# An attention-and-MLP kernel: k of the last six chunks transposed by DMA, in a new fixed order of the work

## The chip, the cores and the metric

The kernel runs on one core of a Trainium2 chip. The metric is the time of one execution in microseconds (us) on the device; the profile adds a trace of one execution. TensorE (PE) does matrix products and transposes, VectorE (DVE), ScalarE (ACT) and GpSimd (POOL) work on elements, SyncE (SP) issues most DMAs. Each engine takes its own instructions in the order in which the program lists them, and waits on semaphores for the others.

## What is computed

A linear attention with a decaying state, and a channel MLP on what it gives. Inputs are r, k, v of shape (4 batches, 8 heads, 768 tokens, 48) in float32.

```python
state = zeros(B, H, 48, 48)
for t in range(768):
    cur = einsum('bhd,bhe->bhde', u * k[t], v[t])
    y[t] = einsum('bhd,bhde->bhe', r[t], state + cur)
    state = w * state + einsum('bhd,bhe->bhde', k[t], v[t])
x = y, heads side by side: (4, 768, 384)
xn = (x - mean(x)) / sqrt(var(x) + 1e-6) * g_ln
out = x + maximum(xn @ w_ch1, 0) @ w_ch2      # 384 -> 1536 -> 384
```

## The kernel before

**Chunks.** The 768 tokens of a batch are cut into 6 chunks of 128, so there are 24 chunks, numbered 0 to 23; chunk i is part i % 6 of batch i // 6. Within a chunk the recurrence becomes products of matrices, and only a state Z passes from a chunk to the next of its batch.

**The words.** Each piece of work has a name with its chunk's number, which this document calls a word. For chunk i they are, in the order of their dependences (lines in brackets):

- `k`, `v`, and `r` for a pair of chunks: loads, issued by SP [180, 186]. Seven buffers each for k and v.
- `sck`: k scaled by powers of w into one of four bf16 buffers [361]; `scr{e}0`, `scr{e}1`: the same for the pair e of r [364].
- `TK`: four TensorE transposes of 128x128 into the PSUM bank `tr` [379]; `kT`: the copy of that bank to SBUF [383]. `TR` and `rT` are the same for r, a pair at a time, in the same bank [394, 400].
- `q`: r times k, elementwise, both transposed [411]; `cc`: its product with u, on PE [438]; `cp` copies that out [449]; `Vb`: v times cp, on POOL [453].
- `at`: eight score products of kT and rT on PE [418]; `A`: the scores times the mask, from PSUM, on DVE [428].
- `vc`: v cast to bf16 [370]; `kv`: the chunk's state product on PE [469, and 460 where Z is carried in by a product]; `S` and `Z`: the state added and decayed [484, 493, 497].
- `y`: A times v, and rT times Z, on PE [521, 509]; `x`: y plus Vb, with the row sum, on DVE [534].
- `xn`: x centred, on ACT or DVE [552, 548]; `sq`, `rs`: the variance and its root [561, 572, 575].
- `ln`, `lc`: xn transposed into xT. For chunks 0 to 7 on TensorE with a copy [605, 617]; from chunk 8 on `lc` is a DMA transpose issued by SP [613].
- `up{g}_{m}`: the first MLP product of group g, part m [630]; `re{g}_{m}`: its relu, on ACT or DVE [644, 646]. Groups 0 to 5 are single chunks, 6 to 14 pairs.
- `dn{i}{m}`: a third of the second MLP product [657] (`dh` for halves of the last chunk [689]); `ot`: the result, on DVE [667]; `st`: its store, issued by SP or ACT [678].
- `w1l`, `w2l`, `w1s`, `w2s`: the MLP's weights loaded in thirds (768 KB each) and scaled or cast [208, 212, 343, 345, 355]. `turn`, `vec`, `uw`, `wl`, `WLZ`, `gn`: small constants at the start; uw is two products of 48x4 on DVE [325].

**The order.** The string ORDER [23 to 67] lists all words once, in an order found beforehand by annealing. A suffix names the engine where there is a choice: `.V` DVE, `.A` ACT, `.G` POOL, `.S` SP. `*n` stands for n filler products on PE. At run time nothing is chosen: each engine gets its words in the order of the string, and SP too, so a DMA that has to wait holds all DMAs behind it on SP. The dependences are declared by `add` [762 to 865].

**KP and QP.** `KP = 24` [590] is the first chunk whose k is not transposed on TensorE, so before all 24 are. For chunks from `QP = 8` to KP, `qp(i)` [405], q reads the PSUM bank of TK itself; for the others it reads the SBUF copy kT:

```python
kT = tk_t[i][:, :HP, :] if qp(i) else kT_t[i][:]
```

For chunks from KP on, `kT` is this on SP, with no TK and no copy; there are four kT buffers in turn:

```python
nc.sync.dma_start_transpose(out=kT_t[i][:], in_=k_bufs[i % NSC].rearrange("p h d -> p (h d)"))
```

Of the kernel before, what the change touches and what calls it, by code (L numbers as in the profile page):

```python
# [20 lines left out]


ORDER = """
r1 k1 k2 Fr0.V k3 v1 v2 w1l2 Fr1.A Fk.A w1l0 scr00.V scr10.G scr11.G r2 scr01.V *18 TR0 rT0.A sck0.V *1 TK0 kT0.A
*1 turn vec uw.V rT1.A sck1.V vc0.V sck2.G *13 at0 *3 TK1 q0.V wl A0 *6 cc0 *1 kv0 kT1.A q1.G WLZ gn TR1 rT2.A *2
y0 at1 rT3.A vc1.A cp0.V Vb0 Z0 sck3.G v3 A1 w1l1 TK2 kT2.V vc2.A cc1 cp1.A kv1 at2 x0 y1 xn0.A ln0 Vb1 q2.G Z1
w1s22.G A2 w1s01.G x1 k4 TK3 kT3.A xn1.A cc2 kv2 lc0.V k5 w1s00.A cp2.V w1s21.G Vb2 scr20.G w1s02.V Z2 w1s20.V v4
w2l0 y2 ln1 lc1.V up0_0 q3.V at3 re0_0.A x2 xn2.V vc3.A up1_0 re1_0.A cc3 up0_2 ln2 re0_2.A sq0 scr21.G A3
w1s12.G lc2.V up1_2 re1_2.V TR2 w1s11.V rT4.V up2_0 y3 sck4.V cp3.A w1s10.A up0_1 re0_1.V Vb3 x3 sck5.G re2_0.A
up2_2 re2_2.V rT5.A TK4 kT4.A q4.G kv3 Z3 up1_1 re1_1.V at4 A4 vc4.G xn3.A w2l1 ln3 up2_1 lc3.A cc4 cp4.A TK5 sq1  # L30
w2s03.V re2_1.A w2s02.G Vb4 up3_2 kv4 w2s01.V rs0 w2s11.G kT5.A w2s00.A y4 x4 xn4.A w2s13.A w2s10.A w2l2 up3_1
re3_1.A w2s20.G at5 dn00 r3 scr31.G q5.V re3_2.V w2s12.V ln4 lc4.V Z4 up3_0 re3_0.A dn01 cc5 v5 w2s23.A w2s22.A
cp5.A Vb5 A5 up4_2 up4_0 w2s21.V dn02 re4_2.A up4_1 scr30.V TR3 sq4 k6 ot0 sq2 sq3 vc5.V y5 r4 re4_1.V k7 rT7.A
rT6.A dn10 dn11 re4_0.A x5 xn5.V ln5 lc5.V dn12 ot1 sck6.G TK6 scr40.G sck7.V up5_0 up5_1 v6 rs1 kT6.A q6.V TK7
kT7.A scr41.V at6 A6 cc6 cp6.A Vb6 dn20 st0.S TR4 q7.V vc6.A kv6 Z6 re5_1.A k8 rT9.A rT8.A dn21 y6 x6 sck8.G at7
A7 dn22 ot2 xn6.A TK8 cc7 cp7.A v7 up5_2 re5_0.A kT8.A re5_2.A vc7.G kv7 S7 Vb7 k10 k9 sck9.G v8 y7 Z7.G x7 xn7.A
r5 dn30 q8 vc8.A at8 A8 v9 k12 dn31 st1.S r6 scr50.G ln6 lc6.V dn32 ot3 cc8 y8 ln7 sq5 lc7.A kv8 S8 dn40 cp8.A
TK9 kT9.A q9 up6_2 dn41 v10 k11 st2.S v12 v13 sq6 scr51.G up6_1 re6_1.A re6_2.A vc9.V sck10.V cc9 cp9.A TR5 Vb8
x8 dn42 rs2 k13 xn8.V lc8 Z8.G scr61.G ot4 Vb9 scr60.G at9 A9 up6_3 kv9 S9 Z9.G dn50 r7 rT11.A rT10.A TK10 q10
sck11.V re6_3.A kT10.A sq7 dn51 y9 x9 up6_4 re6_4.A sck12.V xn9.A lc9 rs3 vc10.G at10 TK11 cc10 q11 kT11.A cp10.A  # L40
up6_0 re6_0.A dn52 A10 up6_5 re6_5.A TR6 st4.A rT13.A rT12.A vc12.G y10 kv10 Vb10 ot5 dn60 at11 dn61 x10 S10
Z10.G cc11 cp11.A A11 xn10.V sck13.G scr70.G v11 vc11.V k15 TK12 kT12.A st5.A dn62 k14 k18 up7_4 at12 re7_4.A
Vb11 up7_5 q12 ot6 re7_5.A sq8 y11 cc12 cp12.A TK13 scr71.G lc10 r8 sq10 dn70 up7_0 up7_2 A12 kT13.V x11 q13
xn11.A lc11 re7_2.V TR7 y12 rT14.A rT15.A vc13.V at13 kv12 Z12 v14 A13 Vb12 up7_1 re7_1.A re7_0.A sq9 sck14.G
# [12 lines left out]
S19 k22 sck22.V v20 y19 x19 rT22.A dn140 up11_1 sq17 re11_1.A dn141 cc20 st13.A cp20.A TK22 kT22.A dn142 at21
up11_0 up11_4 xn18.A vc22.V sck23.V q22 TK23 ot14 xn19.V lc18 lc19 st14.S A21 Z19.G rs8 vc20.G kv20 Vb20 S20
Z20.G re11_0.A kT23.A y20 up11_5 dn150 re11_4.V at23 x20 xn20.V cc21 q23 A23 cp21.A Vb21 re11_5.A up11_2 kv21
dn151 S21 Z21.V up11_3 re11_3.A re11_2.A y21 dn152 sq19 ot15 st15.S cc22 at22 kv22 S22 Z22.G up12_3 dn160 up12_2  # L60
vc23.G A22 x21 cp22.A re12_3.A cc23 dn161 lc20 y23 xn21.V lc21 cp23.A dn162 up12_4 re12_4.A Vb23 re12_2.V up12_1
re12_1.A Vb22 ot16 dn170 up12_5 x23 y22 xn23.A lc23 x22 re12_5.V xn22.V lc22 rs9 dn171 up12_0 dn172 ot17 sq22
up13_0 st17.S re12_0.A up13_5 re13_5.A st7.A re13_0.V dn180 up13_3 re13_3.V dn181 up14_0 re14_0.A sq20 dn182 ot18
up13_4 re13_4.V up13_2 re13_2.A sq23 dn190 up14_3 dn191 up13_1 st18.A re13_1.V dn192 re14_3.A ot19 st19.A up14_4
re14_4.V up14_5 re14_5.A sq21 rs11 rs10 dn200 up14_1 re14_1.A st16.S dn201 up14_2 re14_2.A dn202 ot20 dn210 dh00
dn220 dh01 dn221 dh02 oh0 dn222 ot22 st20.A dn211 dh10 sh0.A st22.A dn212 ot21 st21.S dh11 dh12 oh1 sh1.S
"""


class Planner:  # L70
# [12 lines left out]
    def add(self, name, eng, cost, fn, needs=(), takes=(), gives=(), pri=0, load=0.0, kind=None,  # L83
            alt=None, lands=1.9, after=0.0):

        t = dict(name=name, eng=eng, cost=cost, fn=fn, needs=list(needs), takes=list(takes),
                 gives=list(gives), pri=pri, load=load, kind=kind, alt=alt, lands=lands, end=None,
                 first=(eng, cost), after=after)  # L90
        self.tasks.append(t)
        assert name not in self.by_name, name
        self.by_name[name] = t
# [24 lines left out]
def kernel(  # L118
# [17 lines left out]
    NCH = S // L  # L136
# [106 lines left out]
    NSC, NSR = 4, 2  # L243
# [5 lines left out]
    WLZ = const.tile([P, HP, E2], FP32, name="WLZ")  # L249
# [43 lines left out]
    Fk = const.tile([P, H, D], FP32, name="Fk")  # L293
# [12 lines left out]
    vec = const.tile([P, NR], FP32, name="vec")  # L306
# [3 lines left out]
    wl = const.tile([P, HP], FP32, name="wl")  # L310
# [49 lines left out]
    def scale_k(i, eng):  # L360
        eng.tensor_tensor(out=k_bufs[i % NSC][:, :, :D], in0=k_t[i][:], in1=Fk[:], op=ALU.mult)  # L361
# [10 lines left out]
    def k_bank(i):  # L372
        return "y" if i < 1 else "tr"
# [31 lines left out]
    def qp(i):  # L405
        return QP <= i < KP

# [179 lines left out]
    LNP = 8  # L587
    LNO = 4
    ln_done = []
    KP = 24  # L590
    SZ, QP = 6, 8
    ot_t = {}

# [124 lines left out]
    add = plan.add  # L718
# [22 lines left out]
    for rank, (a, i) in enumerate(seq):  # L741
        pri = 50 - 0.1 * rank
# [19 lines left out]
    for i in range(NT):  # L762
        c = i % NCH
        g, j = tile_group[i]
        last = c == NCH - 1
        p0 = 60 - 2 * i
        e, half = divmod(i, 2)
        add(f"sckb{i}", "", 0.0, None, ([f"TK{i - NSC}"] + ([f"kv{i - NSC}"] if (i - NSC) % NCH < NCH - 1 else [])) if i >= NSC else [], [("sck", i, 1 if last else 2)], pri=p0)
        add(f"sck{i}", "DVE", 0.7, lambda e, i=i: scale_k(i, e), [f"k{i}", "Fk", f"sckb{i}"], [], [("k", i)], pri=p0, after=35 + (i - 6) * PACE if i > 6 else 0.0,
            alt=[("POOL", 1.0)])  # L770
        if not half:
            add(f"scrb{e}", "", 0.0, None, [f"TR{e - NSR}"] if e >= NSR else [], [("scr", e, 1)], pri=p0)
            for t in range(2):
                add(f"scr{e}{t}", "POOL", 1.1, lambda g, e=e, t=t: scale_r(e, t, g), [f"r{e}", f"Fr{t}", f"scrb{e}"], [],
                    [("r", e)], pri=p0, alt=[("DVE", 0.7)])
            add(f"TR{e}", "PE", 0.46, lambda e=e: transposes_r(e), [f"scr{e}0", f"scr{e}1"] + ([f"TK{i - 1}"] if QP < i < KP else []), [("tr", ("r", e), 2)],
                [("scr", e)], pri=p0)
        add(f"rT{i}", "ACT", 0.74, lambda g, i=i: evacuate_r(i, g), [f"TR{e}"] + (["kT0"] if i == 1 else []), [("rT", i, 1)], [("tr", ("r", e))], pri=p0,
            alt=[("DVE", 0.74)])
        if i < KP:  # L780
            add(f"TK{i}", "PE", 0.24, lambda i=i: transposes_k(i), [f"sck{i}"] + ([f"TR{e}"] if qp(i) and i else []), [(k_bank(i), ("k", i), 2 if qp(i) else 1)], [("sck", i)], pri=p0)
# [20 lines left out]
        if not last:  # L802
# [19 lines left out]
            pri=p0 + 2, alt=[("DVE", 0.35)])  # L822
# [78 lines left out]
```

## Time and profile before

| what | value |
|---|---|
| median of 11 runs | 153.42 us (152.78 to 154.24) |
| the profiled execution's own time | 153.73 us |
| its span, first to last instruction | 151.8 us |
| mean granted TensorE clock | 0.989 |
| chain that ended last, by engine | PE 77%, DVE 17%, nothing visible 2%, ACT 1% |
| k transposes on PE (L379) | 96 matmuls, 24 chunks |
| DMA transposes on SP (L613) | 16 |

Busy time counts an engine's instructions; a matmul's end is modelled, so the shares of PE are upper bounds. "Releaser" is what ended an engine's idle time. PEld is the weight load that runs ahead of each matmul. Rows of the timeline give start, duration, engine, source line, operation, output and inputs; the bracket at the end is the idle time before it and what ended that.

### The profile page before, as it was taken

The page shows a single profiled execution, that of the slowest core. Times are in us where ns is not written, and L with a number is a line of the kernel's source. Part 1 is how long each engine was busy: PE and PEld are TensorE (multiplying, and loading weights), DVE is VectorE, ACT ScalarE, POOL GpSimd, SP SyncE. Part 2 cuts the span into 40 slices and gives each one's busy share as a digit, 9 for nine tenths or more (in the row PEclk, how much of TensorE's full clock was granted, in tenths as well). Part 3 has the DMA queues.
Part 4 walks back from the last instruction along what each step waited for, and adds up shares of the span by engine and source line. Part 5 has one row for each costly group of instructions (what it writes and reads, how often), then busy time and mean ns, then how long its engine had stood idle before and what let it go on. Part 6 is the DMA issues. An engine that isn't in the chain of part 4 may idle for free.

```text
span 151.8 us, 4482 instructions
## 1 busy us (share of the span) xinstructions
PE 143.1 (94%) x1778; PEld 112.5 (74%) x1778; DVE 120.8 (80%) x246; ACT 89.0 (59%) x198; POOL 90.1 (59%) x122
## 2 busy tenths in 40 slices
PE   5967899999999999999999999999999999999991
PEld 5856689888677777777778777776867787777770
DVE  5979999998789699899997998679899884535132
ACT  3447567599677676766768554645873526172300
POOL 8087998566687898599817847598384180011200
PEclk9999779999999999999999999999999999999999
DMA  4999998997899994496786898991523121511032
GB/s 97 258 209 324 248 273 160 390 320 166 182 216 238 245 239 122 123 237 126 148 224 150 166 232 166 205 264 58 111 75 101 36 72 30 181 52 52 0 106 107
DMA packets 75563, 25.47 MB, mean 168 GB/s; under 512 B 69648, under 2 KB 74390, under 8 KB 75542
## 3 DMA queue, kind: packets, MB, share of 16 engines
q1 hardware_dynamic: 72966, 23.11, 64.1%
q10 hardware_dynamic: 2480, 2.07, 4.0%
q8 instruction: 14, 0.23, 0.7%
q14 instruction: 7, 0.06, 0.2%
q0 software_dynamic: 96, 0.01, 0.1%
HBM read 18.88 MB, written 4.72 MB: 155 GB/s over the span
## 4 chain that ended last, share of the span: by engine, by line
PE 77%; DVE 17%; issue 2%; ACT 1%; POOL 0%; ACTq 0%; POOLq 0%; DVEq 0%
PE o L657 27%; PE hp L630 26%; PE at L418 4%; DVE A L428 4%; PE tr L379 3%; PE o L259 3%; PE tr L394 3%; PE y L521 2%; PE s L469 2%; PE y L509 2%; DVE vv L370 1%; PE hp L689 1%; DVE x L534 1%; PE hp L657 1%; DVE uwI L325 1%
## 5 line engine op out<-in xcount | busy, mean ns | idle before, releaser
L630 PE MATMUL hp<-xT,w_sb 128*128 128x256 bf16 (+1 forms) x540 | 57.8, 252 | 0.2
L657 PE MATMUL o<-w_sb,hT 128*128 128x384 bf16 x264 | 53.5, 326 | 0.0
L630 PEld LDWEIGHTS <-w_sb 128*128 128x128 bf16 x540 | 43.2, 98 | 7.3 <-ACT w_sb L343 0.4
L644 ACT ACTIVATE hT<-hp 128x512 bf16<-128x512 f32 x54 | 31.9, 598 | 22.1 <-PE hp L630 21.4
L657 PEld LDWEIGHTS <-hT 128*128 128x128 bf16 x276 | 24.5, 97 | 10.5
L428 DVE TENSOR_TENSOR A<-at,mask 128x1024 bf16<-128x1024 f32 x24 | 29.2, 1215 | 1.8 <-PE at L418 1.7
L364 POOL TENSOR_TENSOR sc<-r,Fr 128x384 bf16<-128x384 f32 x19 | 19.7, 1048 | 9.1 <-DMA r<-in_r_dram 9.1
L453 POOL TENSOR_TENSOR Vb<-v,cc 128x384 f32<-128x384 f32 x24 | 20.3, 848 | 7.9 <-ACT cc L449 6.8
L667 DVE SCALAR_TENSOR_TENSOR ot<-o,rs,x 128x384 f32<-128x384 f32 x22 | 13.5, 614 | 8.0 <-PE o L657 7.2
L383 ACT COPY kT<-tr 128x512 bf16<-128x512 bf16 x19 | 11.1, 587 | 12.9 <-PE tr L379 9.9
L400 ACT COPY rT<-tr 128x512 bf16<-128x512 bf16 x20 | 13.9, 744 | 3.8 <-DVE rT L400 1.8
L534 DVE SCALAR_TENSOR_TENSOR x<-y,Vb 128x384 f32<-128x384 f32 x24 | 13.2, 549 | 3.4 <-PE y L521 3.3
L646 DVE TENSOR_SCALAR hT<-hp 128x512 bf16<-128x512 f32 x18 | 12.3, 684 | 4.0 <-PE hp L630 3.8
L561 ACT ACTIVATE sq<-x,sum 128x384 bf16<-128x384 f32 x24 | 14.6, 610 | 1.3 <-DVE x L534 1.3
L361 POOL TENSOR_TENSOR sc<-k,Fk 128x384 bf16<-128x384 f32 x13 | 13.6, 1045 | 0.5 <-DMA k<-in_k_dram 0.5
L572 POOL TENSOR_SCALAR rs<-sqs 128x2 f32<-128x2 f32 x12 | 2.9, 241 | 18.4 <-ACT sq L561 17.8
L493 POOL TENSOR_TENSOR Z<-S,WLZ 128x384 bf16<-128x384 f32 x9 | 9.0, 999 | 7.8 <-DVE S L484 7.8
L379 PE MATMUL tr<-ident,sc 128*128 128x128 bf16 x92 | 9.2, 224 | 2.5 <-DVE sc L361 1.6
L379 PEld LDWEIGHTS <-sc 128*128 128x128 bf16 x96 | 6.6, 100 | 4.2 <-DVE sc L361 2.3
L418 PE MATMUL at<-rT,kT 48*128 48x128 bf16 x192 | 9.5, 219 | 0.0
L575 POOL TENSOR_TENSOR rs<-rs,expo 128x2 f32<-128x2 f32 x12 | 8.5, 710 | 1.0
L521 PE MATMUL y<-vv,A 128*128 128x48 bf16 x192 | 8.8, 185 | 0.2 <-DVE vv L370 0.2
(96 smaller groups left out, 204.7 us busy)
## 6 DMA issues: line engine op xcount, KB each, us to landing
r<-in_r_dram SPq DMA_DIRECT2D x12, 384.0 KB, 4.4
k<-in_k_dram SPq DMA_DIRECT2D x24, 192.0 KB, 4.6
wst<-in_moe_w_ch_dram SPq DMA_DIRECT2D x6, 768.0 KB, 7.5
v<-in_v_dram SPq DMA_DIRECT2D x23, 192.0 KB, 4.3
out_dram<-ot SPq DMA_DIRECT2D x14, 192.0 KB, 2.6
out_dram<-ot ACTq DMA_DIRECT2D x9, 192.0 KB, 2.2
xT<-xn SPq DMA_TRANSPOSE x16, 2.6
v<-in_v_dram ACTq DMA_DIRECT2D x1, 192.0 KB, 3.6
```

Of the source, the lines that this page charges most:

```text
L361: eng.tensor_tensor(out=k_bufs[i % NSC][:, :, :D], in0=k_t[i][:], in1=Fk[:], op=ALU.mult)
L364: eng.tensor_tensor(out=r_bufs[e % NSR][:, j, :, :D], in0=r_t[e][:, :, j * D : (j + 1) * D], in1=Fr[:, j], op=ALU.mult)
L379: nc.tensor.transpose(out=tk_t[i][:, q, :], in_=sc[:, q, :], identity=ident[:])
L400: (eng.copy if eng is nc.scalar else eng.tensor_copy)(out=rT_t[i][:].rearrange("p q (t j) -> p q j t", j=2), in_=tp_t[e][:, :, c * LH : (c ...
L418: nc.tensor.matmul(out=at_t[i][:, par, p, :], lhsT=kT_t[i][p0 : p0 + D, p, :], rhs=rT_t[i][p0 : p0 + D, p, :], start=True, stop=True,)
L428: nc.vector.tensor_tensor(out=A_t[i][:].rearrange("p e q t -> p (e q) t"), in0=at_t[i][:].rearrange("p e q t -> p (e q) t"), in1=mask[:].u ...
L453: nc.gpsimd.tensor_tensor(out=Vb_t[i][:], in0=vf_t[i][:], in1=cc_t[i][:].unsqueeze(2).to_broadcast([P, H, D]), op=ALU.mult)
L534: nc.vector.scalar_tensor_tensor(out=x_t[i][:], in0=y_t[i][:, :C], scalar=1.0, in1=Vb_t[i][:].rearrange("p h d -> p (h d)"), op0=ALU.mult, ...
L561: nc.scalar.activation(out=sq[:], in_=x_t[i][:], func=ACT.Square, bias=sum_t[i][:], scale=-float(C), accum_out=sq_t[e][:, c : c + 1],)
L630: nc.tensor.matmul(out=hp[:, f * gw : (f + 1) * gw], lhsT=w1_sb[:, n, kc, fb * P : (fb + 1) * P], rhs=xT_t[g][:, kc, :gw], start=(kc == 0) ...
L644: nc.scalar.activation(out=out, in_=src, func=ACT.Relu)
L657: nc.tensor.matmul(out=o_t[i][:, :C], lhsT=hT_t[g][:, fk, j * P : (j + 1) * P], rhs=w2_sb[:, fk, :], start=(fk == 0), stop=(fk == FK - 1),)
```

## The change

KP goes from 24 to 18: for chunks 18 to 23 there is no TK, kT is a DMA transpose issued by SP straight from the scaled k, and q reads kT in SBUF. A scaled-k buffer is then free for reuse when that DMA has read it (and kv has). With it the whole string ORDER is replaced by another one: words move and some change engine. Counted over the string, before and after: PE has 24 and 18 TK; fillers 45 and 46; ACT 20 and 14 copies kT, 54 and 51 re, 12 and 15 xn; DVE 18 and 21 re, 11 and 5 sck, 21 and 18 q, 5 and 7 scr; POOL 13 and 19 sck, 3 and 6 q; SP 0 and 6 kT, 14 and 10 st.

The diff, cut; of ORDER the start and the stretch with the six DMA transposes are shown.

```diff
 ORDER = """
-r1 k1 k2 Fr0.V k3 v1 v2 w1l2 Fr1.A Fk.A w1l0 scr00.V scr10.G scr11.G r2 scr01.V *18 TR0 rT0.A sck0.V *1 TK0 kT0.A
-*1 turn vec uw.V rT1.A sck1.V vc0.V sck2.G *13 at0 *3 TK1 q0.V wl A0 *6 cc0 *1 kv0 kT1.A q1.G WLZ gn TR1 rT2.A *2
-y0 at1 rT3.A vc1.A cp0.V Vb0 Z0 sck3.G v3 A1 w1l1 TK2 kT2.V vc2.A cc1 cp1.A kv1 at2 x0 y1 xn0.A ln0 Vb1 q2.G Z1
...
+k1 r1 k2 k3 Fr1.A Fr0.V scr00.V scr01.V w1l2 v1 v2 w1l0 *18 TR0 rT0.V Fk.A sck0.G TK0 sck1.G kT0.A rT1.A vc0.A *1
+turn r2 vec uw.V wl *9 at0 q0.V *5 cc0 A0 scr11.V sck3.V TK1 sck2.G kv0 *10 y0 kT1.A *3 TK2 WLZ at1 A1 kT2.A
+cp0.A scr10.G w1l1 Z0 q1.G TR1 rT2.A at2 rT3.A vc1.A q2.V gn v3 TK3 kT3.A Vb0 x0 A2 vc2.V y1 cc1 cp1.A Vb1 kv1 Z1
+w1s22.A q3.G cc2 xn0.A ln0 at3 w1s01.A cp2.A Vb2 x1 y2 kv2 w1s02.V lc0.V xn1.A ln1 scr20.G w1s00.V w1s21.A
+w1s20.V lc1.V k4 Z2 x2 sq0 scr21.G up0_0 up1_2 A3 w1s11.G re0_0.A xn2.A re1_2.A k5 up1_0 cc3 cp3.V re1_0.A
...
+up8_5 dn91 y14 dn92 cc15 cp15.A Vb15 x14 re8_5.A scr90.G xn14.A q16 rs5 r10 up8_4 re8_4.V lc14 k21 kT18 at16
+up9_5 re9_5.A A16 ot9 y15 up9_2 up9_4 TK17 dn100 x15 sq14 kT17.A kv15 re9_2.V S15 Z15.G dn101 sck19.G at17 dn102
+cc16 vc16.A xn15.A lc15 q17 TR9 st9.A cp16.A scr100.G scr101.G up9_1 ot10 dn110 rT19.V v21 y16 re9_1.V kv16 dn111
+up9_3 kT19 A17 S16 Vb16 sck21.G rT18.A re9_4.A re9_3.V q18.V v18 st10.A up9_0 r11 x16 vc19.V sq12 TR10 cc17
+re9_0.V dn112 ot11 rT20.A cp17.V Z16.V sck20.G kT20 up10_0 at18 A18 q19.V Vb17 sq15 sq13 re10_0.A up10_1 st11.A
+vc18.G dn120 cc18 k23 kT21 v22 y17 dn121 kv18 cp18.A re10_1.A dn122 up10_4 re10_4.A x17 Z18 xn17.A rs6 lc17 ot12
+scr110.V rT21.A st12.A xn16.A lc16 cc19 at19 A19 kv19 S19 y18 up10_2 dn130 scr111.V vc20.V up10_3 Vb18 rs7 x18
+dn131 at20 q20.G A20 sck23.G Z19.G dn132 y19 ot13 k22 sq16 cp19.A Vb19 x19 re10_3.A re10_2.A q21.G up10_5 kT23
+cc20 TR11 at21 vc21.G sq17 re10_5.A cp20.V rT22.V xn18.V A21 dn140 Vb20 y20 sck22.G kT22 q22.G rs8 kv20 dn141 S20
...
-    KP = 24
+    KP = 18
...
-        add(f"sckb{i}", "", 0.0, None, ([f"TK{i - NSC}"] + ([f"kv{i - NSC}"] if (i - NSC) % NCH < NCH - 1 else [])) if i >= NSC else [], [("sck", i, 1 if last else 2)], pri=p0)
+        add(f"sckb{i}", "", 0.0, None, ([f"TK{i - NSC}" if i - NSC < KP else f"kT{i - NSC}"] + ([f"kv{i - NSC}"] if (i - NSC) % NCH < NCH - 1 else [])) if i >= NSC else [], [("sck", i, 1 if last else 2)], pri=p0)
```

## The prediction, made before the changed kernel was run

> **What bounds the kernel now.** I read the page's engine shares first (span 151.8 us), then busy time by stage, then single stretches of the timeline.
>
> ```profile
> PE 143.1 (94%) x1778; PEld 112.5 (74%) x1778; DVE 120.8 (80%) x246; ACT 89.0 (59%) x198; POOL 90.1 (59%) x122
> ```
>
> TensorE (PE) is nearly always busy, but the second engine, VectorE (DVE), has 80% too. So I cut the span into stages; the columns are the stage, its length, and each engine's busy time.
>
> ```profile
> core 0: us, PE busy (x) PEld busy (x) DVE busy (x) ACT busy (x) POOL busy (x), PEclk, DMA share, GB/s
> 7.70:33.10 25.40, 22.30 (x375) 19.10 (x373) 24.19 (x49) 17.07 (x36) 21.24 (x25) 0.93 1.03 276
> 33.10:40.20 7.10, 6.93 (x97) 5.56 (x95) 5.88 (x13) 6.68 (x17) 3.75 (x4) 1.00 0.88 184
> 40.20:105.60 65.40, 65.13 (x841) 49.92 (x839) 57.72 (x111) 42.87 (x94) 49.63 (x63) 1.00 0.82 187
> 105.60:122.10 16.50, 16.25 (x200) 12.50 (x198) 15.36 (x28) 10.05 (x25) 7.74 (x12) 1.00 0.32 82
> 122.10:148.60 26.50, 26.43 (x230) 19.94 (x227) 11.52 (x24) 9.03 (x20) 4.72 (x9) 1.00 0.22 71
> ```
>
> After 33 us PE is full in every stage. Before that DVE is the busiest (24.19 of 25.40). Between 40 and 106 us DVE has only 7.7 us to spare in 65.4.
>
> A busy PE is not a PE at its peak, so I also counted PE's work by the steps from one group's start to the next where nothing waits:
>
> ```profile
> 102.82 0.40 PE L418 MATMUL at<-rT,kT 48*128 48x128 bf16 x8
> 103.15 0.40 PE L379 MATMUL tr<-ident,sc 128*128 128x128 bf16 x4
> 103.38 0.24 PE L438 MATMUL s<-uwI,q 128*128 128x2 bf16 x4
> 103.48 0.36 PE L521 MATMUL y<-vv,A 128*128 128x48 bf16 x8
> ```
>
> The four transposes of one k chunk (L379) take 103.38 - 103.15 = **0.23 us** of PE; the 0.40 shown contains the pipeline's tail, which the next group overlaps. In the same way: at 0.35, cc 0.10, TR 0.45, up and dn 0.66 each, y 0.20 (0.37 with state), kv 0.17 (0.33 with a carried Z), ln 0.17, dh 0.33. Summed over the order's words this is 130.5 us of work. TR0 starts at 7.7 and the last matmul begins at about 148.6, that is 140.9 us, so about 10.4 us are lost. By 33.1 us 17.3 us of work are done in 25.4: **8.1 us are lost there, and only about 2.2 in the 115 us behind it.** From 33 us on a PE microsecond saved is a microsecond of span, as long as DVE keeps up. Below, "mark" means the PE work that stands ahead of a word in the order.
>
> **1. PE work removed.** TK18 to TK23 go: 6 x 0.23 = **-1.38 us**, all of it at marks 75 to 96, in the full stages. Six evacuations kT go too:
>
> ```profile
> L383 ACT COPY kT<-tr 128x512 bf16<-128x512 bf16 x19 | 11.1, 587 | 12.9 <-PE tr L379 9.9
> ...
> xT<-xn SPq DMA_TRANSPOSE x16, 2.6
> ```
>
> Six of these copies are 3.5 us of ScalarE (ACT), which is off the path (59% busy): nothing. The products q18 to q23 read kT in SBUF now, not the PSUM bank tr; the instructions of that line (count, then shortest, median and longest ns) show both forms:
>
> ```profile
> L411 DVE TENSOR_TENSOR q<-rT,tr x16: 406/410/422, 48.6 to 116.6; 128x512 bf16<-128x512 bf16 x16
> ...
> L411 DVE TENSOR_TENSOR q<-rT,kT x5: 418/422/779, 11.8 to 44.2; 128x512 bf16<-128x512 bf16 x5
> ```
>
> 422 against 410 ns on DVE is nothing; q20, q21 and q22 move to GpSimd (POOL).
>
> **2. One stall goes.** TK22 waited in the old order:
>
> ```profile
> 110.01 0.97 DVE L361 TENSOR_TENSOR sc<-k,Fk 128x384 bf16<-128x384 f32 x1 [0.52 <-DMA k<-in_k_dram]
> ...
> 111.04 0.23 PEld L379 LDWEIGHTS <-sc 128*128 128x128 bf16 x4 [0.34 <-DVE sc L361]
> ```
>
> k22 landed late, sck22 followed, and PE stood for about 0.4 us. PE no longer reads sck22 early. Next late is kT22 for at22; see 3. **-0.4 us.**
>
> **3. Six DMA transposes on SP's queue.** The trace has none of this shape. The nearest row is the x transpose of 128x384 shown above: its issue holds SP 1.18 to 2.23 us, median 1.19, and it lands 2.3 to 3.9 us after, median 2.6. For 128x512 the bounds are 0.4 (the shortest plain issue on SP) and 2.23 for the issue, 2.3 and 3.9 x 4/3 = 5.2 for the landing; I take the median row x 4/3, 1.6 and 3.5. From the word kT to its at there are 11.7, 6.9, 8.4, 8.6, 8.6 and 5.4 us of PE work for chunks 18 to 23: each covers 5.2, the last barely. The tile written is that of four kTs before, long read. So no direct wait of PE.
>
> But SP is in order, and a kT waits there for its sck. Behind kT18 stand lc15 and v21, behind kT19 v18 and r11, behind kT20 k23, behind kT21 v22, lc17, lc16 and k22, behind kT23 kT22, then the last lc. v18 is the tight one: already before, the cast of v18 waited for its load,
>
> ```profile
> 98.58 0.50 POOL L370 CAST vv<-v 128x384 bf16<-128x384 f32 x1 [1.65 <-DMA v<-in_v_dram]
> ```
>
> issued at 94.33 (mark 76.9). Now xn15 has mark 73.7 (71.2 before), and lc15, v21 and kT19 (1.2 + 0.6 + 1.6) are ahead of v18, so it issues near mark 78, lands 4.3 later, and with a cast of 0.54 kv18 at 82.6 is late by 0 to 0.6. I take **+0.3**. At chunk 22 POOL runs sck22 and then q22, which waits for kT22's landing; behind q22 stand rs8, vc22, Vb21 and Z21. k22 stands behind lc17 and lc16, whose xn are placed at 84; issued near 88 it lands near 92.6, and this gives q22 done near 98.4 and vc22 near 100, just when kv22 (100.4) wants it: nothing, but 1 to 1.7 us if the landing is at its upper bound.
>
> The Trainium skill, "VectorE: DVE Perf Modes", "The three transpose paths" and "Rules for kernel authors", speaks against the change: a 128x128 bf16 transpose costs 390 ns on TensorE and 1309 ns by DMA, and TensorE is to be used if PSUM will do. By its figures 24 blocks would free 9.4 us of PE and take 31 us of DMA, an estimate; the 0.23 us for four blocks here is far below the first.
>
> **4. The start, reordered.** uw (two tiny products) sits on DVE's path:
>
> ```profile
> 8.07 1.96 POOL L364 TENSOR_TENSOR sc<-r,Fr 128x384 bf16<-128x384 f32 x2 [4.33 <-DMA r<-in_r_dram]
> ...
> 9.03 1.98 DVE L325 TENSOR_TENSOR uwI<-vec 48x4 bf16<-48x4 f32 x2
> ...
> 10.00 0.98 POOL L361 TENSOR_TENSOR sc<-k,Fk 128x384 bf16<-128x384 f32 x1
> ```
>
> Each of the two ends with a POOL instruction (10.0, 11.0), so DVE is held by POOL. The skill's "SBUF — State Buffer", "SBUF: two separate sides", says the two share a port pair that is locked for a whole instruction; the row agrees.
>
> In the new order DVE does scr00, scr01, rT0 (to about 9.1) and uw, while POOL does sck0 (7.3 to 8.35), sck1 (to 9.4), and then wl, which needs uw. So half of uw is free of POOL and it ends near 9.7, not 11.0; then q0 to 10.2, A0 to 11.4, y0 near 11.5 instead of 13.4. It is given back: scr11, two w1s and vc2 now lie on DVE in front of lc1, and w1l2 (768 KB) is loaded ahead of v1 and v2. Going on with row durations I get lc1 done near 21.05 (20.78 before), with up0_0 and at3 behind PE in both orders, and the set up to at4 done near 29.4 against 29.7. **-0.2**, between -1.3 and +1.0, since some 20 handoffs of 0.1 to 0.2 are assumed.
>
> **5. DVE fuller in the middle.** Between marks 24 and 88 (40.2 to 105.6 us before) the new order has on DVE: six more re (683 ns), two vc (797), one each of A (1217), S (552), Z (600), x (630), rT (728), scr (664), two cp (150); fewer: three xn (663), two sck (694), one q (413). That is 10.4 - 3.8 = +6.6 us of durations, about 6.2 after the 6% by which neighbours overlap (61.4 summed, 57.7 busy). So 63.9 us of DVE for about 64.5 of PE. In 70 to 80 us DVE had 9.76 of 10 and PE lost 0.24. At that rate 64 us would cost 1.5; I take **+0.6**, since DVE at 9.34 (60 to 70 us) cost PE nothing. What moves here leaves marks 88 to 104, where DVE gets about 7 us lighter. Bounds: 0 and the +3.3 of rival B.
>
> The tail from dn202 on is the same chain; sq23 and rs11 stand late in the new order, but ACT reaches sq23 some 4 us before oh0 needs it. Nothing.
>
> **Sum:** -1.38 - 0.4 + 0.3 - 0.2 + 0.6 = **-1.1 us**. The profiled execution took 153.73 (span 151.8 and 1.9 around it), 0.3 over the median of the runs, 153.42. From the median: **152.3 us**. Faster and slower count from 0.3% (0.46 us), about what a measurement of this kernel can tell from no change.
>
> **Rivals.**
> A, the forecast: PE stays the bound, 152.3. For it: 2.2 us lost in 115.
> B, **DVE becomes the bound** at marks 24 to 88. Of its 7.7 us of idle time only 0.6 may remain. DVE takes its work in order and so waits for PE now and then; if half the idle time stays (3.9), the stage needs 63.9 + 3.9 = 67.8, 2.4 over 65.4. With the rest of the sum (-0.5 for the TKs beyond, -0.4) it gives 154.9. It makes the kernel slower from 2.4 us of idle on. Against it: DVE that is late finds its inputs ready and idles less.
> C, **the transposes' queue eats the gain**: v18 late by 0.6, the chain k22, sck22, kT22, q22, Vb21 by 0.8, DVE 0.6: about 0 in all, 153.4.
> D, the earlier y0 is kept in good part (1.3 of 1.9): 151.0.
>
> **How the numbers follow.** A 0.46 (0.41 of it faster, 0.05 within), B 0.22, C 0.17 (0.14 within, 0.03 slower), D 0.15. So faster 0.56, same 0.19, slower 0.25. The range takes in most of D and B: 150.7 to 154.9.
>
> **What would show it.** Right: 72 matmuls at L379; the last PE stage as long as before; PE work from 33 us on shorter by 1.4. Wrong: PE idle before y, kv or dn released by DVE between 40 and 106 us (B); POOL idle on DMA for v18 or kT22, or PE at L418 waiting for a transpose (C); PE's first up groups a microsecond earlier or later than 19.8 (D, or the walk in 4).

## The result, and the profile after

| | before | changed |
|---|---|---|
| median | 153.43 us (50 runs) | **155.06 us** (154.24 to 157.06, 13 runs) |
| ratio to before, 95% interval | | 1.0105 [1.0085, 1.0126] |
| the profiled execution's own time | 153.73 us | 154.67 us |
| its span | 151.8 us | 152.6 us |
| mean granted TensorE clock | 0.989 | 0.978 |

The forecast was 152.3, in a range of 150.7 to 154.9. The changed kernel is 1.6 us slower, not 1.1 faster. Executions more than 1.5% above the fastest of their kernel count in the medians of this document and not in its ratios.

The transposes did leave TensorE: L379 has 72 matmuls in place of 96. The page's first line of the changed kernel:

```profile
PE 142.4 (93%) x1755; PEld 112.4 (74%) x1755; DVE 123.7 (81%) x247; ACT 85.5 (56%) x190; POOL 94.9 (62%) x123
```

PE is busy 0.7 us less and the span is 0.8 longer. Busy time by stage, over the stretches that the prediction showed (length, then each engine's busy time, then the granted clock):

```profile
7.70:33.10 25.40, 22.23 (x362) 19.49 (x359) 22.65 (x44) 19.02 (x41) 19.54 (x24) 0.87 1.06 289
33.10:40.20 7.10, 6.24 (x96) 5.13 (x95) 6.40 (x10) 4.80 (x14) 4.88 (x6) 1.00 0.93 200
40.20:105.60 65.40, 64.23 (x821) 49.39 (x819) 60.50 (x116) 39.80 (x91) 49.25 (x62) 1.00 0.91 185
122.10:148.60 26.50, 26.50 (x233) 20.36 (x232) 13.28 (x27) 9.62 (x21) 5.26 (x9) 1.00 0.20 64
```

Three things differ. The clock of the first stage is 0.87 (0.93 before). PE has 0.86 us to spare between 33 and 40 us, where it had 0.17. In the long stage DVE is busy 60.50 us. That row is the same stretch of time and not of work: between the marks of the forecast's stage, 24 and 88, which are 42.1 and 108.1 us here, DVE is busy 61.57 of 66.00, 3.9 more than before and 2.3 less than forecast. The last stage is full in both.

Shares by stage do not say how much each stage lost, since work moved between them. So I made a ledger with the prediction's own steps: the start of a word, less the start of TR0, less the PE work ahead of it (its mark), is the time that PE has lost by then.

| mark | lost before, us | lost after, us | more by |
|---|---|---|---|
| 12.1 | 7.90 | 8.76 | 0.86 |
| 24.5 | 8.56 | 10.58 | 2.02 |
| 49.5 | 9.02 | 11.52 | 2.50 |
| 62 | 9.78 | 12.20 | 2.42 |
| 86 | 9.88 | 12.53 | 2.65 |
| 124 | 10.24 | 12.57 | 2.33 |

2.33 lost less 1.38 of work removed is +0.95 from TR0 on. TR0 itself starts 0.33 us earlier in the changed kernel (7.35 for 7.68), and the two spans differ by 0.8, the two executions by 0.94. **Nearly all of it is lost by mark 24, in the first 42 us; the six DMA transposes come at 92 us and later.** Behind mark 86 the new order loses 0.04 where the old one lost 0.36.

The six transposes themselves, by tile kT in the changed kernel: count and shortest, median, longest issue in ns; who waited; time to landing.

```profile
L387 SPq DMA_TRANSPOSE kT<-sc x6: 1190/1228/1816, 92.1 to 113.2; - x6
...
  POOL q L411: 2.6, 1
...
DMA to landing us min/median/max: 2.4/3.7/5.0
```

PE is not in the list: no score product waited for a transpose in this execution. q22 waited 2.6 us on POOL, and PE was not held by that.

**The start.** uw was freed of POOL, both halves of it where the forecast had one. DVE's timeline of the changed kernel (start, duration, engine, line):

```profile
9.02 0.33 DVE L325 TENSOR_TENSOR uwI<-vec 48x4 bf16<-48x4 f32 x2
...
11.43 1.35 DVE L361 TENSOR_TENSOR sc<-k,Fk 128x384 bf16<-128x384 f32 x1
```

0.33 us in place of 1.98, and y0 began at 11.11 in place of 13.39. But then sck3 took 1.35 us where an undisturbed one takes 0.56, with scr10 on POOL until 12.37 and q1 right behind it. PE stood, between 12.5 and 17.9 us, 0.99 ahead of at2, 0.66 ahead of y1, 0.38 ahead of kv1 and 1.26 ahead of cc2, which wanted Z1, on DVE behind the cast vc2 (0.93). Then the granted clock fell. PE in windows of 2 us, before:

```profile
17.00:19.00 2.00, 1.96 (x25) 0.53 0.75 157
19.00:21.00 2.00, 1.89 (x29) 0.62 0.92 225
21.00:23.00 2.00, 2.00 (x42) 1.00 1.17 328
```

and in the changed kernel (busy, number of matmuls, granted clock):

```profile
17.00:19.00 2.00, 1.15 (x17) 0.50 1.08 359
19.00:21.00 2.00, 2.00 (x27) 0.50 1.15 247
21.00:23.00 2.00, 2.00 (x21) 0.50 0.71 127
```

Half clock lasts from 17.10 to 20.52 before (3.42 us) and from 16.42 to 23.25 after (6.83 us, twice that). Two groups of up in it, up0_0 and up1_2, took 1.28 us each in place of 0.66. A mean clock of 0.978 over the span is two such stretches, 0.989 one. All runs of the changed kernel show 0.973 to 0.978, while runs of the kernel before show from none to two. The Trainium skill, "TensorE: Matmul & The Clock Gate", "What's actually happening", gives a free-running window of 3413 ns after whose idleness PE runs at half rate; both lengths here are multiples of it. But PE was not idle in the 3.41 us ahead of the fall, it was busy 1.63 of them in the changed kernel (below) and 2.16 in the kernel before. In the 3.41 us ahead of those, from 10.28 to 13.69, the kernel before had been busy only 2.04, and its clock stayed up. So the runs bear out the length and not the condition.

```profile
13.01:16.42 3.41, 1.63 (x32) 1.00 1.05 311
```

**Marks 12 to 24.** PE waited 0.78 us ahead of ln4 and 0.53 ahead of ln5. The first of them in the timeline of the changed kernel:

```profile
32.94 1.15 POOL L411 TENSOR_TENSOR q<-rT,kT 128x512 bf16<-128x512 bf16 x1
...
33.12 1.18 DVE L548 TENSOR_SCALAR xn<-x,sum 128x384 bf16<-128x384 f32 x1
...
34.36 0.34 PE L605 MATMUL tr<-ident,xn 128*128 128x128 bf16 x3 [0.73 <-DVE xn L548]
```

xn4 begins on DVE just after q5 has begun on POOL, and ends only after it. By itself it takes 0.5 us (0.52 in a run below). DVE waited for POOL inside the instruction. xn5 takes 0.92 us in the same way, beside scr40.

### The profile page after: what moved, and what is told of

It is laid out like the page before. It is cut to its first block, busy times and chain, and to the rows that moved or that the text cites. A ratio compares the mean times of both kernels' runs of the same rounds, so it can differ in the third digit from the quotient of the medians.

```text
span 152.6 us, 4438 instructions
## 1 busy us (share of the span) xinstructions
PE 142.4 (93%) x1755; PEld 112.4 (74%) x1755; DVE 123.7 (81%) x247; ACT 85.5 (56%) x190; POOL 94.9 (62%) x123
## 4 chain that ended last, share of the span: by engine, by line
PE 76%; DVE 17%; issue 3%; ACT 1%; POOL 1%; POOLq 0%; DVEq 0%; ACTq 0%
PE hp L630 28%; PE o L657 24%; DVE A L428 4%; PE at L418 4%; PE y L521 3%; PE tr L394 2%; DVE xn L548 2%; PE s L469 2%; DVE vv L370 2%; PE y L509 2%; DVE x L534 2%; PE o L259 2%; PE tr L379 2%; DVE sc L361 1%; PE hp L689 1%
## 5 line engine op out<-in xcount | busy, mean ns | idle before, releaser
L630 PEld LDWEIGHTS <-w_sb 128*128 128x128 bf16 x540 | 44.3, 100 | 7.1
L644 ACT ACTIVATE hT<-hp 128x512 bf16<-128x512 f32 x51 | 30.1, 597 | 24.2 <-PE hp L630 24.0
L657 PEld LDWEIGHTS <-hT 128*128 128x128 bf16 x276 | 24.5, 97 | 10.8 <-issue 0.2
L361 POOL TENSOR_TENSOR sc<-k,Fk 128x384 bf16<-128x384 f32 x19 | 19.8, 1046 | 3.9 <-ACT Fk L304 3.4
L646 DVE TENSOR_SCALAR hT<-hp 128x512 bf16<-128x512 f32 x21 | 14.4, 688 | 6.3 <-PE hp L630 6.3
L364 POOL TENSOR_TENSOR sc<-r,Fr 128x384 bf16<-128x384 f32 x17 | 18.4, 1095 | 0.7 <-DMA r<-in_r_dram 0.7
L552 ACT ACTIVATE xn<-x,sum 128x384 bf16<-128x384 f32 x15 | 9.2, 612 | 4.9 <-DVE x L534 3.4
L383 ACT COPY kT<-tr 128x512 bf16<-128x512 bf16 x13 | 7.6, 585 | 5.9 <-PE tr L379 3.6
L493 POOL TENSOR_TENSOR Z<-S,WLZ 128x384 bf16<-128x384 f32 x7 | 7.4, 1061 | 3.1 <-DVE S L484 3.1
L418 PEld LDWEIGHTS <-kT 48*128 48x128 bf16 x192 | 5.5, 95 | 5.1 <-issue 2.0
L411 POOL TENSOR_TENSOR q<-rT,kT 128x512 bf16<-128x512 bf16 x6 | 7.4, 1225 | 2.6 <-DMA kT<-sc 2.6
```

Of the source, the lines that this page charges most:

```text
L364: eng.tensor_tensor(out=r_bufs[e % NSR][:, j, :, :D], in0=r_t[e][:, :, j * D : (j + 1) * D], in1=Fr[:, j], op=ALU.mult)
L418: nc.tensor.matmul(out=at_t[i][:, par, p, :], lhsT=kT_t[i][p0 : p0 + D, p, :], rhs=rT_t[i][p0 : p0 + D, p, :], start=True, stop=True,)
L630: nc.tensor.matmul(out=hp[:, f * gw : (f + 1) * gw], lhsT=w1_sb[:, n, kc, fb * P : (fb + 1) * P], rhs=xT_t[g][:, kc, :gw], start=(kc == 0) ...
L644: nc.scalar.activation(out=out, in_=src, func=ACT.Relu)
L646: nc.vector.tensor_scalar(out=out, in0=src, scalar1=0.0, scalar2=None, op0=ALU.max)
L657: nc.tensor.matmul(out=o_t[i][:, :C], lhsT=hT_t[g][:, fk, j * P : (j + 1) * P], rhs=w2_sb[:, fk, :], start=(fk == 0), stop=(fk == FK - 1),)
```

## The experiments

Times are medians, ratios are to the kernel before on the same chip with the 95% interval. "Lost" is the ledger's figure.

### The DMA transposes in the old order

The first theory was that the transposes are worth their 1.4 us and the new start loses it (T1); the rival, that SP's queue takes the gain (T2). **e1_old_order_dma**: KP = 18 in the old order, each kT right behind its sck.

```diff
-sck18.G ... TK18 kT18.A
+sck18.G kT18
```

So for all six, with v20 and sck23 ahead of sck22.

> The old order with the DMA transposes put into it by hand: KP = 18, no TK18 to TK23, each kT right behind its sck (sck23 moved ahead of sck22 so that kT23 has time). Theory 1 (the transposes do what was reckoned, the loss is in how the new order runs its first 70 us): PE loses 1.38 us of work and the 0.4 us stall at TK22, so 151.3 to 152.2 us, and L379 shows 72 matmuls. Theory 2 (DMA transposes cost more than they save: SP's queue, DMA traffic, late kT): no gain, 153.4 us or more, with PE or POOL idle on kT.

**e2_before_plus_dma**: the kernel before, with the six transposes added behind the same sck into a tile that nobody reads; all 24 TK stay.

```diff
+nc.sync.dma_start_transpose(out=t_[:], in_=k_bufs[i % NSC].rearrange("p h d -> p (h d)"))
```

> The kernel before, all 24 TK kept, and for chunks 18 to 23 one more DMA transpose of the scaled k behind each sck, into a tile that nothing reads. This adds the transposes' cost alone. Theory 1: 153.2 to 153.9 us, as before. Theory 2: the transposes must cost about the 1.6 us that the change lost and the 1.4 us that it saved on PE, so about 156 us, and at least 154.5.

Measured: e1 166.38 us, 1.0783 [1.0725, 1.084]; e2 164.25, 1.0676 [1.0623, 1.073]. By the ratios T1 as it stood missed by 13 us: placed there, the transposes cost 10 us even when nobody reads them and no PE work is saved (e2), and the kernel is 12 us slower with the saving (e1). SP's timeline in e1:

```profile
82.00 0.53 SPq L677 DMA_DIRECT2D out_dram<-ot  x1
85.81 1.88 SPq L386 DMA_TRANSPOSE kT<-sc  x1
87.77 1.21 SPq L612 DMA_TRANSPOSE xT<-xn  x1
```

and PE's:

```profile
90.20 1.16 PE L629 MATMUL hp<-xT,w_sb 128*128 128x256 bf16 x6 [3.51 <-DMA xT<-xn]
```

From 82.5 to 85.8 SP stands before kT18, whose sck18 is only made by then. Behind it is the x transpose of chunk 13, which went out at 82.08 in the kernel before and at 87.77 here, and PE waits 3.51 us for it. What is late here is no k transpose, it is what stands behind one on SP. SP stands before kT20 in the same way, until 110.06, and PE loses 3.1 us more at 116 to 119, where the chain of what it waits for leads back over the landings of two k transposes.

**e5_old_order_dma_timed** and **e8_before_plus_dma_timed** are e1 and e2 with the six at places where the trace of before has the scaled k ready: behind k19, v22, k23, st12 and, two of them, v20, with a few words moved for them (sck20 and sck23; in e5 also q19, q21, q22). In e8 the six are the unread ones.

```diff
-k19 ... v22 ... k23 ... st12 ... sck22 v20 ... sck23
+k19 kT18 ... v22 kT19 ... k23 kT20 ... st12 kT21 ... sck23 sck22 v20 kT23 kT22
```

> KP = 18 in the old order again, but each kT stands on SP's queue at a place where, by the trace of before, its sck has ended (behind k19, v22, k23, st12 and v20), sck20 and sck23 are earlier on their engines, and q19, q21, q22 later on VectorE. Theory 1: what cost 11 us in the first two experiments was SP held by a kT that waited for its sck, with the x transposes and loads behind it; without that the six chunks save 1.4 to 1.8 us: 151.3 to 152.3 us. Theory 2 (the transposes themselves are too slow or disturb other DMAs): 153.4 us or more.

> The kernel before with the six unread DMA transposes of the second experiment, at the places on SP's queue that the run beside this one uses for kT (and sck20, sck23 and v20 moved likewise); all 24 TK stay on PE. Theory 1: the 11 us of the second experiment were the waits on SP's queue, so 153.2 to 154.0 us now. Theory 2: still 155 us or more, as six transposes more are issued in either.

Measured: e5 155.14, 1.0075 [1.0044, 1.0107]; e8 155.47, 1.0132 [1.0091, 1.0173]. Most of the loss has gone, but not all: by the ratios 1.2 us is left in e5 and 2.0 in e8. SP in the kernel before, then in e8:

```profile
91.78 1.21 SPq L613 DMA_TRANSPOSE xT<-xn  x1
...
95.54 1.95 SPq L180 DMA_DIRECT2D r<-in_r_dram  x1
```

```profile
93.53 1.21 SPq L616 DMA_TRANSPOSE xT<-xn  x1
...
99.74 0.58 SPq L179 DMA_DIRECT2D r<-in_r_dram  x1
```

The x transpose of chunk 15 is 1.8 us late and the load of r11 4.2, after two transposes of k. PE loses 3.8 us between 91 and 115 us in the profiled execution of e8 (157.00 us, above its median), where the kernel before loses 0.5. Half of it lies ahead of dn130, which waits for an ot on DVE; and that ot waits for an earlier store, which stands behind r11 on SP, goes out 2.8 us later than before (100.36 for 97.58) and lands 5.29 us after:

```profile
100.36 5.29 DMA out_dram<-ot
...
105.76 0.62 DVE L670 SCALAR_TENSOR_TENSOR ot<-o,rs,x 128x384 f32<-128x384 f32 x1 [2.05 <-DMA out_dram<-ot]
```

**e4_old_then_new**: the order of e1 up to dn70 (mark 52), which holds none of the six, and behind it all other words in the new order.

> KP = 18; the order of the first experiment up to about 52 us of PE work (dn70), and behind it the words that are left in the changed kernel's order. Theory 1: the new order loses PE time only ahead of this point, so 151.3 to 152.4 us, about as the first experiment. Rival (the later stretch with the DMA transposes and the fuller VectorE loses): 154 us or more.

Measured: 155.63, 1.0141 [1.0106, 1.0176]. The seam alone costs about 5 us between marks 53 and 58, so the total tells nothing of the two halves. But from mark 60 on, where the six transposes lie, only 0.4 to 0.6 us is lost. This and the ledger answer T2 for these two executions: at the new order's places the queue costs PE nothing to speak of, and at the old order's it costs 2 to 10 us (e8, e2). That it is not free at the new places either, once PE comes earlier or SP later, e11, e14 and e16 show.

### The clock

**e3_new_order_warm**: the changed kernel with 53 filler products on PE, so that it does not idle at the start.

```diff
-... WLZ at1 A1 ... TR1 rT2.A ... TK3 kT3.A ... cc1 cp1.A ... kv1 Z1
+... WLZ at1 *5 A1 ... TR1 *14 rT2.A ... TK3 *9 kT3.A ... cc1 *5 cp1.A ... kv1 *20 Z1
```

> The changed kernel with 53 filler products on PE, in five places between 11.8 and 18 us where PE stood idle (behind at1, TR1, TK3, cc1 and kv1). Theory 1, in its part on the clock: the granted clock was at half for 6.8 us there against 3.4 us before, and the fillers hold it up; the first up groups no longer take 1.28 us each, and the time falls by 0.8 to 1.7 us to 153.4 to 154.3. Rival (VectorE is late by itself, so a faster PE only waits longer): the clock stays up, the time stays at 154.7 to 155.3.

**e9_before_warm**: the same for the kernel before, with 26 fillers (11 behind at1, 11 behind cc1, 4 behind y1).

```diff
-y0 at1 rT3.A ... cc1 cp1.A ... y1 xn0.A
+y0 at1 *11 rT3.A ... cc1 *11 cp1.A ... y1 *4 xn0.A
```

> The kernel before with 26 filler products on PE between 13.7 and 17.1 us (behind at1, cc1 and y1), where PE stood idle ahead of its 3.4 us at half clock. If half the clock is paid for in time also here, 152.4 to 153.1 us; if VectorE sets the pace there, 153.2 to 153.7 us.

Measured: e3 153.77, 1.0029 [1.0002, 1.0056], 1.29 under the changed kernel; e9 153.45, 0.9981 [0.995, 1.0012]. PE in windows of 2 us, in e3:

```profile
17.00:19.00 2.00, 2.00 (x45) 1.00 1.10 351
19.00:21.00 2.00, 1.47 (x25) 1.00 1.18 277
```

Full clock. Up to cc2 PE runs as in the changed kernel (17.89 us, and 17.92 there); up2_1, at mark 12.7, starts at 27.84 in place of 29.01. All that was changed is work that nobody reads, so the cold stretches are worth 1.1 us by the traces, 1.3 by the medians and, by the intervals, 0.6 to 1.7.

The median of e9 hides two groups. In six executions the clock stays at 0.997 to 1.0, and five of them took 152.2 to 152.6 us, the sixth 154.0; in the other six it is 0.988 or 0.989, and they took 153.4 to 153.8. So the fillers hold the clock there only half of the time, and the expectation of 152.4 to 153.1 fits where they do. But the kernel before by itself takes the same 153.3 at a clock of 0.985 to 0.989 and at 0.997 to 1.0 (medians of 32 and 20 of its runs), so what the five gain by stays open.

### DVE, POOL and the handoffs

**e15_new_order_q5_dve**: the changed kernel with only q5 moved, from POOL to DVE.

```diff
-kT5.A q5.G re3_2.A ... w2s12.V w2s13.A
+kT5.A re3_2.A ... w2s12.V q5.V w2s13.A
```

> The changed kernel with q5 on DVE in place of GpSimd, behind w2s12, and nothing else. If xn4 is slow (1.18 us in place of 0.4) because q5 on GpSimd holds DVE, the wait of 0.8 us ahead of ln4 goes and with it 0.5 to 0.8 us of time: 154.2 to 154.6. Rival: it only shifts the wait to the next handoff (dn11 to ln5), 154.9 to 155.2.

Measured: 155.97, 1.0172 [1.0117, 1.0227]. The expectation missed; it is not faster at all. Three executions took 155.0 us and three 156.9 to 157.5. The wait ahead of ln4 has gone, as foreseen: xn4 takes 0.52 us now. But q5 itself takes 1.21 now, beside scr31 on POOL (34.40 to 35.50), and a cast of w2 that stands behind it on DVE is late for PE. DVE, then PE, in e15:

```profile
33.55 0.52 DVE L547 TENSOR_SCALAR xn<-x,sum 128x384 bf16<-128x384 f32 x1
...
34.57 1.21 DVE L410 TENSOR_TENSOR q<-rT,kT 128x512 bf16<-128x512 bf16 x1
```

```profile
37.70 0.48 PE L656 MATMUL o<-w_sb,hT 128*128 128x384 bf16 x2 [0.24 <-DVE w_sb L354]
```

By mark 24.5 it has lost 10.42 us, the changed kernel 10.58. As the rival had it, the wait moves to the next handoff, though to another one (cc5 and not ln5). The profiled execution is one of the first three, 155.02, the same as the changed kernel; what makes the others 2 us slower stays open.

**e7_new_order_warm_port**: e3, with q5 on DVE and xn5 on ACT.

```diff
-kT5.A q5.G re3_2.A ... w2s12.V w2s13.A ... rT7.A rT6.A ... x5 xn5.V ln5
+kT5.A re3_2.A ... w2s12.V q5.V w2s13.A ... rT7.A ... x5 xn5.A rT6.A ln5
```

> The third experiment (new order with fillers, 153.77 us), and besides q5 from GpSimd to VectorE (behind w2s12) and xn5 from VectorE to ScalarE (ahead of rT6). In its trace PE waited 0.78 us for xn4, which took 1.18 us on VectorE beside q5 on GpSimd, and 0.54 us for xn5, 0.92 us beside scr40. If GpSimd holding VectorE's port is the cause of these two waits: xn4 takes 0.3 to 0.6 us, both waits of PE shrink, and the time falls by 0.6 to 1.2 us to 152.6 to 153.2. If VectorE is late for want of time, the waits move to the next group and it stays at 153.5 to 154.0.

**e11_new_order_warm_handoffs**: e7 and six more moves, read from the waits in e7's trace.

```diff
-w1s21.A w1s20.V lc1.V ... sq0 ... re0_0.A ... cp5.A ... vc5.V ... x5 xn5.A rT6.A ln5 lc5.V r4 dn12
+w1s21.A w1s20.A lc1.V ...  re0_0.A sq0 ... cp5.A vc5.A ... x5 xn5.A rT6.A r4 dn12 ln5 lc5.V
-vc10.V ... re6_3.A ... TK12 q12 kT12.V
+re6_3.A vc10.A ... TK12 kT12.A q12
```

> The fillers and the q5/xn5 moves of the run before, and six handoffs that its trace shows late are mended by hand: w1s20 and vc5 and vc10 go from DVE to ACT, kT12 goes from DVE to ACT ahead of q12, sq0 goes behind re0_0, ln5 stands behind dn12. Their waits in that trace are up0_0 0.74 us, y5 0.29, dn11 0.84, kv10 0.40, y10 0.23, up7_1 0.55: 3.05 in all. Theory (the loss of the new order is late handoffs on DVE and a cold clock at the start, and the DMA transposes are worth their 1.4 us of TensorE): most of it comes off, as every one of them lies where TensorE is full behind it; 151.0 to 152.0 us, 1 to 2 us below the 153.03 of that run and below both kernels. Rival (the transposes' queue or another bound holds the end, so that waits removed come back behind): 152.7 to 153.3.

Measured: e7 153.03, 0.9986 [0.9966, 1.0007]; e11 **151.62**, 0.9864 [0.9824, 0.9904]. In e7 the wait ahead of ln4 is gone; ahead of ln5 it has grown from 0.53 to 0.84 us, released by rT6 on ACT. e11 beats both kernels, by 1.4% and 2.2%, with the same six DMA transposes at the same places. The ledger of e11 has 9.30 lost at mark 62, where e7 has 10.40, e3 11.45 and the changed kernel 12.20.

Behind mark 62 e11 loses 1.50 us, though, and the changed kernel 0.37. With PE two microseconds earlier kT18, 5.93 us from issue to landing, is late for q18 on DVE; re9_0 stands behind q18, and PE waits 1.04 us for the bank that re9_0 empties. DVE, then PE, in e11:

```profile
95.40 0.75 DVE L410 TENSOR_TENSOR q<-rT,kT 128x512 bf16<-128x512 bf16 x1 [0.72 <-DMA kT<-sc]
```

```profile
97.88 0.82 PE L629 MATMUL hp<-xT,w_sb 128*128 128x256 bf16 x6 [0.99 <-DVE hT L645]
```

DVE idled 0.72 us for that transpose, so some 0.7 of the 1.4 us saved on PE is given back here.

**e13_new_order_handoffs**: e11 without its fillers.

> As the run above, without a filler added: the changed kernel with q5, xn5 and the six handoffs moved alone. If clock and handoffs add up (1.3 us for the fillers was measured on the changed kernel), it is 1.3 us above the run above: 152.3 to 153.3. Rival: with the handoffs mended TensorE idles less at the start and no second window at half clock comes, then it is within 0.4 us of the run above.

Measured: 154.34 (153.04 to 155.63), 1.0035 [1.0, 1.007]. Above the forecast, so the two parts do not add: fillers are worth 1.3 us on the changed kernel and 2.7 on this one. All its runs show a clock of 0.973 to 0.978, yet they spread over 2.6 us; what spreads them at the same mean clock stays open. The clock falls at 15.28 us in its trace, ahead of all the words that were moved.

**e16_new_order_warm_handoffs2**: e11 with rT6 on DVE, and re9_0 ahead of x16 and vc19.

```diff
-x5 xn5.A rT6.A ... r11 x16 vc19.V ... cc17 re9_0.V
+x5 rT6.V xn5.A ... r11 re9_0.V x16 vc19.V ... cc17
```

> On top of the run of 151.62 (fillers, q5 and xn5, six handoffs): rT6 on DVE behind x5 in place of ACT (rT6 on ACT kept the PSUM bank that ln5 wants until 39.5), and re9_0 ahead of x16 and vc19 on DVE (up10_1 waited for its bank until 97.8). The two waits are about 1.1 (dn12 to TK6) and 1.0 us. Theory: both come off in good part, as TensorE is full behind them: 150.3 to 151.2. Rival: the next wait behind them takes it up, 151.4 to 151.9.

Measured: 151.50, 0.989 [0.9856, 0.9923]: the same as e11. The wait of 1.04 us ahead of up10_1 went, and 0.59 appeared ahead of kv18; ahead of ln5 and TK6 0.89 of 1.15 stayed. The rival was right again, and here it is the queue: kv18 waits for the cast of v18, which on SP stands behind kT19 and landed 4.07 us after its issue. POOL in e16:

```profile
99.44 0.76 POOL L369 CAST vv<-v 128x384 bf16<-128x384 f32 x1 [0.38 <-DMA v<-in_v_dram]
```

### What the removed PE work is worth

**e12_new_order_k_on_pe**: KP = 24 in the new order, the six TK put back by hand, with copies on ACT.

```diff
-kT18 ... kT19 ... rT18.A ... q18.V ... vc19.V ... TR10 cc17
+rT18.A TK18 kT18.A q18.V ... vc19.V ... cc17 TK19 kT19.A q19.V TR10
```

> The changed order with the transposes put back: KP is 24, TK18 to TK23 stand on TensorE near their chunks' scores, their copies kT on ACT, q18 to q23 all on DVE reading the PSUM bank, rT21 and rT23 a little earlier so that the one bank comes free. No DMA transposes k. If the saving of TensorE work is real where the changed order has it, this is 1.4 us above the changed kernel (155.06), 156.2 to 157 with a wait or two for the shared bank. Rival (the DMA transposes cost SP's queue what they save on TensorE): 154.6 to 155.3, the same as the changed kernel or faster.

Measured: 162.72, 1.0567 [1.052, 1.0613], far above both expectations. What PE waited for in e12:

```profile
PE tr L394 <- DVE q L411: 2.3, 2, 1.2
...
PE tr L379 <- ACT rT L400: 1.4, 1, 1.4
```

TR and TK share the bank tr, and in this order its readers q and rT come late for that. These two are 3.7 us of the 7.7 lost; the rest I did not follow. So this run does not measure the work alone, and says nothing on step 1.

**e14_new_order_more_pe** puts only the work back: for chunks 18 to 23 five of the eight score products are done twice, with the same result.

```diff
-        for p in range(HP):
-            for par in range(2):
+        pairs = [(p, par) for p in range(HP) for par in range(2)]
+        for p, par in (pairs[:5] if i >= KP else []) + pairs:
```

> The changed kernel with TensorE work of the removed size put back: for chunks 18 to 23 the first five of the eight score products are done twice (the same result), 5/8 of 0.35 = 0.22 us each, 1.31 in all; no copy, no bank, no queue comes with it. If step 1 of the prediction holds (TensorE is the bound there, and a microsecond of its work is a microsecond of span) this is 1.1 to 1.5 us above the changed kernel: 156.2 to 156.6. Rival: the stage has slack that takes it up, then it stays within 0.4 us of 155.06.

Measured: 156.08, 1.0176 [1.0143, 1.021], 1.02 us over the changed kernel. The added work is less than 1.31: a doubled group takes 0.49 us to the next group's start, the others 0.33, so 0.98 in all. The difference of the ratios, 0.7%, is 1.1 us, give or take 0.6 by their intervals. So the work is paid for in full, just under the expectation because its size was overrated, and the rival's 0.4 is at the edge of the interval. In the profiled execution the ledger has 2.12 us more lost at the end than the changed kernel's: 0.98 are the work and 1.03 a wait of kv18 for v18, which went out 1.6 us later than in the changed kernel (98.28 for 96.68). POOL, then PE, in e14:

```profile
102.86 0.50 POOL L370 CAST vv<-v 128x384 bf16<-128x384 f32 x1 [1.21 <-DMA v<-in_v_dram]
```

```profile
103.42 0.33 PE L470 MATMUL s<-vv,sc 128*128 128x96 bf16 x4 [0.88 <-POOL vv L370]
```

## Why the prediction was wrong

**Step 1, -1.38: right.** The work left and PE is the bound there; e14 pays 1.0 to 1.1 us for 0.98 put back. For the evacuations and q no wait of PE shows.

**Steps 2 and 3, -0.4 and +0.3: together -0.3.** The stall at TK22 went, and behind mark 86 the loss fell from 0.36 to 0.04. v18 did no harm to PE there. The bounds for issue and landing held in the changed kernel (1.19 to 1.82 and 2.4 to 5.0 us for 0.4 to 2.23 and 2.3 to 5.2), the 3.5 taken for the landing was near the median of 3.7, and the 1.6 for the issue was above its 1.23. Rival C, the queue, did not come. In part that is luck: with PE later than forecast there was time to spare. In e14 and e16 kv18 waits 1.0 and 0.6 us for v18, the tight place that step 3 had named, and in e11 kT18 lands after 5.9 us, over the upper bound, and gives back some 0.7. What the queue costs at other places, 10 us, e2 shows.

**Step 5, +0.6: right in size by luck.** Between marks 24.5 and 86 the new order loses 0.63 us more (1.95 for 1.32). But DVE is not full there: 61.57 of 66.00 us, and not the 63.9 of about 64.5 that the step had. What PE loses are single late handoffs: 0.40 behind kv10 and 0.55 behind up7_1, where kT12 stands on DVE behind A11 and q12. Rival B, DVE as the bound of the stage, did not come, and in e11 these two are gone.

**Step 4, -0.2: this is the step that failed**, with the stretch behind it that was put at nothing. The start lost 0.86 us more by mark 12, and another 1.16 by mark 24. In the walk's own terms the set up to at4 was done at 30.11 us, and not at 29.4, for 29.7 before. Both have a reason in the working.

- The walk took durations from rows and put the new words one behind the other up to at4. It had uw and y0 right, each even 0.4 earlier than it said. It did not have the operations that POOL then holds (sck3 1.35 us), and let the early y0 carry on; PE stood behind it instead, and the clock fell for two windows in place of one. Nothing in the sum had a price for the clock, though the row of before, 0.93 in that stage, showed that it was near. e3 prices it at 1.1 to 1.3 us, more than the 0.86: with the clock held up the new start would not be behind the old one as it ran, with its one window.
- Marks 12 to 24 had no term at all. The walk ended near at4, and step 5 began at mark 24. There xn4, which was on ACT before, and xn5 wait on DVE for POOL, and PE waits for them, 0.78 and 0.53 us. e3, at full clock, has the same two waits, 0.78 and 0.54.

By the ledger: -1.38 (step 1), -0.32 (2 and 3), +0.63 (5) and +2.02 (4 and the stretch behind it) give +0.95. With -0.2 for the last the sum would have been -1.27. (Rival D's 151.0 is 151.2 by its own terms, -1.3 in place of -0.2.) The medians differ by more than the profiled executions, 1.6 for 0.94: 0.3 of it is the profiled run of before, which lies over its median, and 0.4 that of the changed kernel, which lies under its own.

So of the 2.02 about 1.1 is the clock, 1.2 the handoffs behind mark 12, and the rest of the start gained some 0.3. The medians do not add as neatly: fillers alone give 1.29, handoffs on top of them 2.15 (two of which lie behind mark 24), handoffs alone 0.72, and together 3.44. Why the handoffs are worth so much more with the fillers stays open.

## What to carry to other kernels

When a change brings a whole new order with it, price the new order from the first word to the last, also where the named change isn't: here the edit earned its 1.4 us of PE work and the order's first 42 us spent it. Keep a ledger of time lost against work done for both kernels, and let no stretch be without a term. Where the clock already dips, as in the kernel before, price a start that leaves PE waiting with the clock too: here that was 1.1 us. And a DMA transpose on a queue in order is worth only the place it stands in: its slack goes when PE gets faster, as in e11.

## What the runs showed of the hardware

- The clock alone was worth 1.1 to 1.3 us: 6.83 us at a granted clock of 0.5 in the profiled execution, a mean of 0.973 to 0.978 in all runs, and 53 products that nobody reads took 1.29 us off (e3). The Trainium skill, "TensorE: Matmul & The Clock Gate", "What's actually happening", puts the penalty of the ramp under 1% of a typical kernel's span; 1.29 of 155.06 is 0.8%, for two cold windows behind the ramp.
- A vector instruction held by POOL takes two to six times as long: xn4 1.18 us beside q5 and 0.52 without; uw 0.98 each before and 0.16 after. The Trainium skill, "SBUF — State Buffer", "SBUF: two separate sides", says that a shared port pair is locked for a whole instruction, and the rows agree. What it is worth can't be read from the row: e15 removed the one of xn4 and gained nothing.
- Six DMA transposes of 128x512 that nobody reads cost 10 us at one set of places (e2) and 2 at another (e8). Their own issue is 1.2 us each at the median in both; what PE waits for, where it was followed, is what stood behind them on SP. From issue to landing one took 2.4 to 6.1 us (changed kernel, e11, e16).
